# Storing the raw first up product and applying its activation beside the first down product; moving the second layer's weight combinations

## The chip, the cores and the metric

The kernel runs on 1 core of one Trainium2 chip. The metric is device time in microseconds (us) of one execution. Engines are named as in the profile: PE (matrix products, with PEld for the loads of its weights), DVE, ACT, POOL (element-wise work) and SP (here it only issues DMAs). ACT issues DMAs too: the stores.

## What is computed

```python
def _attn_ref(q, k, v, p):
    p_packed = sm_attn(p, k, v)
    return sm_attn(q, p_packed, p_packed)

def _moe_ref(x, w_in, w_out):
    h = x @ w_in
    g = h * np.cos(h)
    return g @ w_out

def _moe2_ref(x, w_in, w_out):
    h = x @ w_in
    g = np.where(h >= 1, h, np.where(h <= -1, 0.0, (h + 1) ** 2 / 4))
    return g @ w_out
```

Batch 8, 8 heads, 576 tokens, head width 64, 32 packed rows; 4608 tokens by 512 in all, and an inner width of 2048 in both layers. `reference` is attention, then the first layer (`moe_`), then the second (`moe2_`). Weights arrive as 64-bit floats and are cut to 32 bits on the chip.

## The kernel before, in words

A 32-bit value is cut by `split` (L66) into a high part, copied by ACT (L67), and a low part, a subtraction on POOL or DVE (L68). A product is three matmuls: high by high, high by low, low by high (`TERMS`).

**Attention phase with the first up product.** For each batch `n`, `stage1` and `stage2` make scores and softmaxes; the second attention's packed values are folded into the weights (`form_M`, `load_M` make `M[n, c]`), so that `up(n, hf, fp)` (L593) forms a 128x2x288 piece of h in 12 matmuls. There are 128 such items: 8 batches, 2 halves of the tokens, 8 pairs of inner blocks. The loop over `items` (L952) is written by hand: after each item it takes one step in each of the streams "load", "wt", "mat", "att" (Python generators), so these set what stands between two items. A scheduler then orders each engine's queue; `tc.high_priority` and `issue_after` shift pieces of it. The stream "wt" holds `cut_w_in` at first, and from batch 6 on `cut_w_out` (L502): 16 rows of blocks of the first layer's output weights, each brought in raw by SP, converted by `convert` (L124: ACT, four on DVE, POOL) and split.

h stays in one of three PSUM buffers `hps` until the activation h*cos(h) is done: `act_a` (L610) has ACT round h/2pi to an integer (L614) and DVE subtract it (L615); `act_b` (L620) has ACT take the sine (L623) and DVE multiply by h from PSUM (L624). The result goes to HBM as `g1T`.

**First down product** (`run_down1`, L775). 128 items of 24 matmuls (L792), each on one tile `g` loaded from `g1T` by SP, split by ACT and DVE (L786). Every eighth item ends a block: sums leave PSUM (L801, L803) and are stored as `yT`. After each item `step("wt")` takes one step of `combine` (L530): the second layer's products use seven combinations of blocks (a 2x2 scheme with 7 instead of 8 products, `ORDER_UP`, `KS`), and `combine` forms these from the weights. It has 16 units, 8 for `w_in2` (stored as `su`) and 8 for `w_out2` (`sd`). A unit is two raw loads (SP), two `convert`, four additions on DVE (L559 to L562), four `split` into tiles `pl`, and seven stores (SP).

**Second up product** (`run_up2`, L820). 8 batches times 4 pairs of inner blocks; each is a cycle of seven products of 12 matmuls (L743). Results leave PSUM by ACT (L716) and DVE (L721), go through `activate` (L724: ACT twice, DVE L729) and are stored as `gT`. Products that share a PSUM bank X, Y or Z add onto it, so PE waits there for DVE or ACT. `load_y` brings in the next batch once per four cycles and forms its seven sources on POOL and ACT.

**Second down product** (`run_down2`, L850): the same scheme with `sd`; 8 batches of 7 products of 48 matmuls (L891).

## Time and profile before

| what | us |
|---|---|
| median of 3 runs (1750.95 to 1758.61) | 1755.22 |
| the profiled execution's own time | 1760.71 |
| its span, first to last instruction | 1758.9 |
| PE busy in the span | 1596.1 (91%) |
| DVE busy | 1126.6 (64%) |
| ACT busy | 918.6 (52%) |
| POOL busy | 522.9 (30%) |

The mean granted clock of PE over the span is 0.945 of full speed. PE's busy share is of little use by itself: its instructions overlap, and one that runs at the lower clock is as busy as one at full speed. PEld's share is close to 100% where PE runs at its full rate. The stages follow one another, so they are read apart: the attention phase from 0 to 551 us, the first down product to 1015, the second up product to 1378, the second down product to the end.

### The profile page before, as it was taken

What the parts mean: (1) busy time and instruction counts of PE and PEld (TensorE: products, weight loads), DVE (VectorE), ACT (ScalarE), POOL (GpSimd) and SP (SyncE); (2) the same over time, 40 slices, a digit from 0 to 9 for tenths busy, and PEclk for the clock granted to TensorE, in tenths of its full rate; (3) what the DMA queues carried; (4) which work ended last, traced back from release to release, by engine and by line L of the source; (5) the groups of instructions that cost most, each with busy time, mean ns of one, the idle gap of its engine ahead of it and who ended that gap; (6) DMA issues with size and microseconds to landing.
All of it is one profiled execution on the core that took longest, in us unless ns stands there. A gap on an engine that the chain in (4) does not pass through costs nothing. (4 is left out here: it accounts for less than half of the span.)

```text
span 1758.9 us, 28668 instructions
## 1 busy us (share of the span) xinstructions
PE 1596.1 (91%) x10846; PEld 1524.1 (87%) x10846; DVE 1126.6 (64%) x1611; ACT 918.6 (52%) x1478; POOL 522.9 (30%) x376
## 2 busy tenths in 40 slices
PE   8679888878764998998999999999999799999998
PEld 6458777777664998988899999999999799999998
DVE  4887456547898665767522246666666597778775
ACT  3467678757665333333322246766666444444443
POOL 2763233333464463545300114444443000000000
PEclk7779999989987999999999999999999899999999
DMA  7566785646657898887744443333335954444430
GB/s 227 154 195 199 216 239 191 214 138 196 199 168 240 259 344 286 266 277 236 216 122 116 164 188 135 130 136 135 129 135 219 387 168 130 137 133 135 135 109 34
DMA packets 174539, 326.96 MB, mean 186 GB/s; under 512 B 16192, under 2 KB 70464, under 8 KB 170816
## 3 DMA queue, kind: packets, MB, share of 16 engines
q1 hardware_dynamic: 120128, 230.73, 42.8%
q10 hardware_dynamic: 54272, 94.39, 14.4%
q8 instruction: 85, 1.39, 0.3%
q14 instruction: 54, 0.44, 0.1%
HBM read 184.55 MB, written 130.02 MB: 179 GB/s over the span
## 5 line engine op out<-in xcount | busy, mean ns | idle before, releaser
L68 DVE TENSOR_TENSOR r<-g,r 128x576 fp32r<-128x576 f32 x352 | 286.9, 824 | 232.6 <-ACT r L67 227.1
L67 ACT ACTIVATE r<-g 128x576 fp32r<-128x576 f32 x352 | 239.2, 683 | 312.5 <-PE psZ L891 70.6
L604 PE MATMUL hps<-at,m 128*128 128x288 f32 x1536 | 255.5, 322 | 52.9 <-DVE u L624 39.9
L604 PEld LDWEIGHTS hps<-at,m 128*128 128x128 f32 x1536 | 233.0, 207 | 73.6 <-issue 40.8
L792 PE MATMUL psZ<-r,wo 128*128 128x288 f32 x1536 | 213.8, 300 | 12.0 <-ACT r L67 6.5
L792 PEld LDWEIGHTS psZ<-r,wo 128*128 128x128 f32 x1536 | 209.9, 191 | 15.1 <-DVE r L68 7.9
L891 PE MATMUL psZ<-r,sw 128*128 128x288 f32 x1152 | 159.6, 297 | 2.7 <-DVE r L68 1.8
L891 PEld LDWEIGHTS psZ<-r,sw 128*128 128x128 f32 x1152 | 156.4, 189 | 3.2 <-DVE r L68 2.0
L729 DVE SCALAR_TENSOR_TENSOR t<-hh,t 128x576 f32<-128x576 f32 x128 | 113.7, 889 | 69.8 <-ACT t L728 69.7
L792 PE MATMUL psX<-r,wo 128*128 128x288 f32 x768 | 130.0, 303 | 27.3 <-ACT r L67 21.8
L68 POOL TENSOR_TENSOR ty<-td,ty 128x576 fp32r<-128x576 f32 x32 | 52.0, 1630 | 306.5 <-ACT ty L67 306.5
L792 PEld LDWEIGHTS psX<-r,wo 128*128 128x128 f32 x768 | 112.5, 192 | 31.3 <-ACT r L67 22.7
L727 ACT ACTIVATE t<-hh,half 128x576 f32<-128x576 f32 x128 | 98.7, 772 | 61.8 <-DVE hh L721 48.7
L792 PE MATMUL psY<-r,wo 128*128 128x288 f32 x768 | 125.4, 299 | 0.0
L615 DVE SCALAR_TENSOR_TENSOR u<-hps,u 128x576 f32<-128x576 f32 x128 | 95.3, 747 | 45.0 <-ACT u L614 44.6
L68 POOL TENSOR_TENSOR m<-ml,m 128x512 fp32r<-128x512 f32 x64 | 85.0, 1341 | 128.9 <-ACT m L67 116.5
L624 DVE TENSOR_TENSOR u<-hps,u 128x576 f32<-128x576 f32 x128 | 94.8, 746 | 34.9 <-ACT u L623 34.9
L891 PE MATMUL psX<-r,sm 128*128 128x288 f32 x768 | 107.1, 299 | 9.2 <-ACT r L67 9.0
L891 PEld LDWEIGHTS psX<-r,sm 128*128 128x128 f32 x768 | 104.9, 190 | 9.7 <-ACT r L67 9.2
L743 PE MATMUL psZ<-ty,sw 128*128 128x288 f32 x768 | 111.8, 296 | 0.1
L792 PEld LDWEIGHTS psY<-r,wo 128*128 128x128 f32 x768 | 111.6, 191 | 0.0
L623 ACT ACTIVATE u<-u,halfpi 128x576 f32<-128x576 f32 x128 | 98.1, 771 | 25.5 <-DVE u L615 25.3
(158 smaller groups left out, 2783.4 us busy)
## 6 DMA issues: line engine op xcount, KB each, us to landing
g1T<-u ACTq DMA_DIRECT2D x128, 288.0 KB, 3.2
g<-g1T SPq DMA_DIRECT2D x128, 288.0 KB, 4.1
gT<-t ACTq DMA_DIRECT2D x128, 288.0 KB, 2.1
g<-gT SPq DMA_DIRECT2D x128, 288.0 KB, 3.3
raw<-in_moe_w_in SPq DMA_DIRECT2D x32, 512.0 KB, 6.1
raw<-in_moe_w_out SPq DMA_DIRECT2D x32, 512.0 KB, 4.7
su<-pl SPq DMA_DIRECT2D x56, 256.0 KB, 5.0
sd<-pl SPq DMA_DIRECT2D x56, 256.0 KB, 4.1
```

The costliest lines, as they stand in the source:

```text
L67: nc.scalar.activation(out=hi, in_=src, func=AF.Copy)
L68: (eng or nc.gpsimd).tensor_tensor(out=lo, in0=src, in1=hi.bitcast(F32), op=ALU.subtract)
L604: nc.tensor.matmul(out=hps[:, j, :HB], lhsT=m[:, w, G, cs], rhs=x[:, G, y], start=(G == 0 and i == 0), stop=(G == 1 and i == 2),)
L615: nc.vector.scalar_tensor_tensor(out=u, in0=h, scalar=1 / (2 * PI), in1=ki, op0=ALU.mult, op1=ALU.subtract)
L623: nc.scalar.activation(out=u, in_=u, func=AF.Sin, scale=2 * PI, bias=halfpi)
L624: nc.vector.tensor_tensor(out=u, in0=h, in1=u, op=ALU.mult)
L727: nc.scalar.activation(out=t, in_=h, func=AF.Relu, scale=0.5, bias=half)
L729: nc.vector.scalar_tensor_tensor(out=t, in0=h, scalar=1.0, in1=t, op0=ALU.max, op1=ALU.min)
L743: nc.tensor.matmul(out=ps[:, i], lhsT=s[:, d, w, cs], rhs=t[:, d, y], start=first and d == n == 0, stop=d == 1 and n == 2, skip_group_chec ...
L792: nc.tensor.matmul(out=acc[d // 2][:, d % 2], lhsT=wo[f // 4, w][:, f % 4, ds], rhs=r[:, y, k], start=f == n == 0, stop=f == NFT - 1 and n ...
L891: nc.tensor.matmul(out=ps[:, j], lhsT=s[:, f % 4, w, j * 128:j * 128 + 128], rhs=r[:, y, k], start=first and f == n == 0, stop=f == 7 and ...
```

## The change

1. `up` no longer applies the activation. One instruction copies h from PSUM (ACT for even `fp`, DVE for odd) and the raw h is stored as `h1T`.
2. `run_down1` loads h, and applies the activation there in SBUF: `act_a` three items ahead, `act_b` two, `split` one.
3. `combine` leaves `run_down1`. The units of `w_in2` go to the attention phase, in the stream "wt", from item 33 on (`cut_w_out` gets a stream of its own, "wo"); those of `w_out2` go to the second up product, one step after each product on X or Y.
4. A unit is spread over 11 steps instead of 6. Its tiles shrink: two raw buffers instead of four, one `pl` instead of two; the sums `pc` share a buffer with raw. `p1` has two buffers instead of three, `u` three instead of four. `load_v` takes the second half of v into the one buffer, later than before.

```diff
-    def combine(units):
-        def load(src):
-            raws = []
-            for x in range(2):
-                raw = prep[0].tile([128, 2, 256, 2], I32, tag="raw", name="raw", bufs=4)
...
+    def combine(units, slow):
+        def load(src, x):
+            raw = prep[0].tile([128, 2, 256, 2], I32, tag="raw", name="raw", bufs=2)
...
-                convert(raw, a[:, o])
+                convert(raw, a[:, o], last_act)
+                yield
                 store()
-                yield
-            if u + 1 < len(units):
-                nxt = load(units[u + 1][0])
-            s = prep[0].tile([128, 4, 256], F32, tag="pc", name="pc")
+            s = prep[0].tile([128, 4, 256], F32, tag="raw", name="pc", bufs=2)
+            raws = [load(following, 0)] if following else []
...
+            yield
             for k, n in ((0, 2), (2, 1), (3, 2), (5, 2)):
-                hl = prep[0].tile([128, 2, 2, 256], F32R, tag="pl", name="pl", bufs=2)
+                hl = prep[0].tile([128, 2, 2, 256], F32R, tag="pl", name="pl")
...
-                split(hl[:, 0, :n], hl[:, 1, :n], x)
-                store()
+                with behind(last_act):
+                    split(hl[:, 0, :n], hl[:, 1, :n], x)
...
                 yield
+                store()
+                if k < 5:
+                    for _ in range(slow - 1):
+                        yield
+            if following:
+                raws.append(load(following, 1))
+            yield
...
-        HS[n, hf, fp] = hps[:, :, :HB]
...
+        u = wk.tile([128, 2, HB], F32, tag="u", name="u", bufs=3)
+        with tc.high_priority(offset=PRI_MAIN):
+            if fp % 2:
+                nc.vector.tensor_copy(out=u, in_=hps[:, :, :HB])
+            else:
+                last_act[:] = [nc.scalar.activation(out=u, in_=hps[:, :, :HB], func=AF.Copy).ins]
+        late_store(h1T[fp, :, 2 * n + hf], u)
...
     def run_down1():
...
-        streams["wt"].append(combine([*units_up(), *units_down()]))
...
+        def act_a(i):
+            if i < B * 16:
+                t = turns[i] = pt.tile([128, 2, HB], F32, tag="t", name="t")
+                ki = t.bitcast(I32)
+                nc.scalar.activation(out=ki, in_=G1[i], func=AF.Copy, scale=1 / (2 * PI), bias=0.25)
+                nc.vector.scalar_tensor_tensor(
+                    out=t, in0=G1[i], scalar=1 / (2 * PI), in1=ki, op0=ALU.mult, op1=ALU.subtract
+                )
+
+        def act_b(i):
+            if i < B * 16:
+                t = turns[i]
+                nc.scalar.activation(out=t, in_=t, func=AF.Sin, scale=2 * PI, bias=halfpi)
+                nc.vector.tensor_tensor(out=t, in0=G1.pop(i), in1=t, op=ALU.mult)
+
+        def part(i):
+            if i < B * 16:
+                r = parts[i] = dn1["r"].tile([128, 2, 2, HB], F32R, tag="r", name="r1")
+                split(r[:, 0], r[:, 1], turns.pop(i), nc.vector)
+
+        for i in (0, 1, 2):
+            act_a(i)
+            if i:
+                act_b(i - 1)
+        part(0)
         for i in range(B * 16):
...
-            g = G1.pop(i)
-            r = dn1["r"].tile([128, 2, 2, HB], F32R, tag="r", name="r1")
-            split(r[:, 0], r[:, 1], g, nc.vector)
+            load_h1(i + 7)
+            part(i + 1)
+            act_b(i + 2)
+            act_a(i + 3)
+            r = parts.pop(i)
...
-            step("wt")
...
+        prep[:] = [pool("prep")]
+        last_act.clear()
+        streams["wt"].append(combine(units_down(), 2))
...
                     product_up(p, f, o, st)
+                    if o[0] != "Z":
+                        step("wt")
...
         if i == n_first + 1:
             drain("wt")
...
+            prep[:] = late
+            streams["wt"].append(combine(units_up(), 2))
         if n == B - 2 and fp == 0 and hf == 0:
-            streams["wt"].append(cut_w_out())
+            streams["wo"].append(cut_w_out())
...
```

How the queues stand is shown at three places. The first is DVE in the middle of the attention phase: `hps` is the PSUM piece of h, `u` its copy in SBUF, `pa`, `raw` and `pc` are the tiles of `combine`. Before:

```order
L615 SCALAR_TENSOR_TENSOR u<-hps,u 128x576
L238 TENSOR_REDUCE mx_3304<-s_3303 128x1
L624 TENSOR_TENSOR u<-hps,u 128x576
L239 TENSOR_SCALAR mx_3304<-mx_3304 128x1
L615 SCALAR_TENSOR_TENSOR u<-hps,u 128x576 x2
L247 TENSOR_SCALAR rs_3392<-sm_3390 128x1
L248 RECIPROCAL rs_3392<-rs_3392 128x1
L249 TENSOR_SCALAR s_3303<-s_3303,rs_3392 128x576
L624 TENSOR_TENSOR u<-hps,u 128x576
```

and now:

```order
L609 COPY u<-hps 128x576
L131 TENSOR_SCALAR pa<-raw 128x512
L132 SCALAR_TENSOR_TENSOR pa<-raw,pa 128x512
L343 STREAM_TRANSPOSE x<-psB 128x288
L135 TENSOR_SCALAR raw<-pa 128x512
L136 SCALAR_TENSOR_TENSOR raw<-raw 128x512
L609 COPY u<-hps 128x576
L551 TENSOR_TENSOR pc<-pa 128x256
L552 TENSOR_TENSOR pc<-pa 128x256
L553 TENSOR_TENSOR pc<-pc,pa 128x256
L554 TENSOR_TENSOR pc<-pa,pc 128x256
```

Two DVE instructions per item became one per two items, and the combination's ten stand between them.

The second place is DVE from the last items to the start of the first down product; `w_...` is a block of the first layer's output weights, `h_...` a loaded tile of raw h. Before:

```order
L131 TENSOR_SCALAR w_4661<-raw 128x512
L624 TENSOR_TENSOR u<-hps,u 128x576
L132 SCALAR_TENSOR_TENSOR w_4661<-raw,w_4661 128x512
L135 TENSOR_SCALAR raw<-w_4661 128x512
L136 SCALAR_TENSOR_TENSOR raw<-raw 128x512
L131 TENSOR_SCALAR pa<-raw 128x2x256
L132 SCALAR_TENSOR_TENSOR pa<-raw,pa 128x2x256
L135 TENSOR_SCALAR raw<-pa 128x512
L131 TENSOR_SCALAR pa<-raw 128x512
L136 SCALAR_TENSOR_TENSOR raw<-raw 128x512
```

and now:

```order
L131 TENSOR_SCALAR w_4632<-raw 128x512
L132 SCALAR_TENSOR_TENSOR w_4632<-raw,w_4632 128x512
L135 TENSOR_SCALAR raw<-w_4632 128x512
L136 SCALAR_TENSOR_TENSOR raw<-raw 128x512
L773 SCALAR_TENSOR_TENSOR t<-h_4661,t 128x576
L773 SCALAR_TENSOR_TENSOR t<-h_4663,t 128x576
L781 TENSOR_TENSOR t<-h_4661,t 128x576
L773 SCALAR_TENSOR_TENSOR t<-h_4665,t 128x576
L781 TENSOR_TENSOR t<-h_4663,t 128x576
L773 SCALAR_TENSOR_TENSOR t<-h_4667,t 128x576
L68 TENSOR_TENSOR r_4829<-t,r_4829 128x576
L781 TENSOR_TENSOR t<-h_4665,t 128x576
```

Where one block of weights (its last three rows) and the first combination stood between the last item and the first split, the last copy of h now stands sixteen rows, four blocks of weights, ahead of the first L773, and the activation of the first items stands ahead of the first split.

The third place is DVE in the second up product; `p_...` is the copy of X1's result, `q`, `u`, `hh` are sums out of PSUM, `t` is the activation. Before, one cycle:

```order
L729 SCALAR_TENSOR_TENSOR t<-hh,t 128x576
L721 TENSOR_TENSOR hh<-psZ,q 128x576
L729 SCALAR_TENSOR_TENSOR t<-hh,t 128x576
L721 TENSOR_TENSOR hh<-psY,u 128x576
L729 SCALAR_TENSOR_TENSOR t<-hh,t 128x576 x2
L721 TENSOR_TENSOR hh<-psZ,p_10458 128x576
L721 TENSOR_TENSOR u<-psZ,p_10609 128x576
L721 TENSOR_TENSOR q<-psY,p_10609 128x576
L729 SCALAR_TENSOR_TENSOR t<-hh,t 128x576 x2
L721 TENSOR_TENSOR hh<-psZ,q 128x576
L721 TENSOR_TENSOR hh<-psY,u 128x576
```

and now:

```order
L708 TENSOR_TENSOR q<-psY,p_10379 128x576
L716 SCALAR_TENSOR_TENSOR t<-hh,t 128x576
L131 TENSOR_SCALAR pa<-raw 128x512
L132 SCALAR_TENSOR_TENSOR pa<-raw,pa 128x512
L135 TENSOR_SCALAR raw<-pa 128x512
L136 SCALAR_TENSOR_TENSOR raw<-raw 128x512
L708 TENSOR_TENSOR hh<-psZ,q 128x576
L716 SCALAR_TENSOR_TENSOR t<-hh,t 128x576
L708 TENSOR_TENSOR hh<-psY,u 128x576
L551 TENSOR_TENSOR pc<-pa 128x256
L552 TENSOR_TENSOR pc<-pa 128x256
L553 TENSOR_TENSOR pc<-pc,pa 128x256
```

The conversions and additions of `combine` stand between the sums that free PE's banks.

## Rows read from the trace of the kernel before

**Rows 1.** Busy time by stretch: start:end, length, busy us by engine (instructions), PE clock, DMA.

```profile
core 0: us, PE busy (x) PEld busy (x) DVE busy (x) ACT busy (x) POOL busy (x), PEclk, DMA share, GB/s
68.00:216.00 148.00, 123.04 (x645) 103.78 (x644) 106.79 (x162) 96.45 (x169) 65.58 (x51) 0.85 0.63 192
216.00:445.00 229.00, 196.34 (x1152) 172.20 (x1152) 136.60 (x220) 162.23 (x277) 79.94 (x64) 0.94 0.65 199
445.00:551.00 106.00, 72.67 (x420) 65.75 (x419) 95.41 (x137) 71.04 (x113) 58.80 (x44) 0.89 0.57 182
...
569.00:860.00 291.00, 270.94 (x1921) 264.14 (x1919) 194.12 (x273) 110.51 (x186) 143.09 (x99) 0.97 0.85 275
860.00:1015.00 155.00, 154.73 (x1150) 154.73 (x1151) 39.99 (x54) 36.40 (x55) 5.61 (x4) 0.99 0.49 148
...
1040.00:1350.00 310.00, 309.95 (x2323) 309.47 (x2322) 194.84 (x251) 216.63 (x326) 121.44 (x74) 1.00 0.37 133
```

**Rows 2.** The chain that ended last, second down product: start us, us, what.

```profile
1427.20 6.40 PE psZ L891 x48
```

**Rows 3.** Waits of PE, 68 to 551 us: waiting, releaser, us, times, longest.

```profile
PE hps L604 <- DVE u L624: 39.9, 26, 6.0
PE psB L454 <- ACT cp L460: 10.1, 7, 3.6
```

**Rows 4.** Waits of PE, 445 to 551 us.

```profile
PE hps L604 <- DVE u L624: 29.6, 17, 6.0
```

**Rows 5.** Waits of all engines, 568 to 860 us.

```profile
ACT pl L67 <- DMA sd<-pl: 41.0, 21, 5.0
ACT pl L67 <- DMA su<-pl: 27.7, 13, 5.2
...
PE psX L792 <- ACT r L67: 21.8, 4, 19.1
```

**Rows 6.** Waits in SP's DMA queue, 568 to 860 us.

```profile
SPq L543 <- POOL pl L68: 74.4, 44, 4.8
```

**Rows 7.** Groups by line, whole run: out<-in, forms, count, busy us, mean ns, idle before.

```profile
L67 ACT ACTIVATE r<-g 128x576 fp32r<-128x576 f32 x352 | 239.2, 683 | 312.5 <-PE psZ L891 70.6 <-PE psY L792 65.8 <-PE psZ L792 54.4
...
L729 DVE SCALAR_TENSOR_TENSOR t<-hh,t 128x576 f32<-128x576 f32 x128 | 113.7, 889 | 69.8 <-ACT t L728 69.7
...
L623 ACT ACTIVATE u<-u,halfpi 128x576 f32<-128x576 f32 x128 | 98.1, 771 | 25.5 <-DVE u L615 25.3
L615 DVE SCALAR_TENSOR_TENSOR u<-hps,u 128x576 f32<-128x576 f32 x128 | 95.3, 747 | 45.0 <-ACT u L614 44.6
L624 DVE TENSOR_TENSOR u<-hps,u 128x576 f32<-128x576 f32 x128 | 94.8, 746 | 34.9 <-ACT u L623 34.9
...
L614 ACT ACTIVATE u<-hps 128x576 int32<-128x576 f32 x128 | 81.8, 644 | 39.1 <-PE hps L604 34.3 <-DMA g1T<-u 1.6 <-DVE e L267 0.8
...
L623 ACT ACT_TABLE_LOAD x15 | 19.2, 1283 | 0.3
...
L801 DVE COPY o<-psZ 128x576 f32<-128x576 f32 x8 | 6.0, 752 | 16.5 <-PE psZ L792 16.5
```

**Rows 8.** Busy time, 551 to 863 us, of tiles pa, pl; lines L129, L136, L139.

```profile
551.00:863.00 312.00, 90.94 (x160) 16.55 (x32) 89.08 (x64) 0.94 0.84 275
...
551.00:863.00 312.00, 36.55 (x64) 85.67 (x64) 0.94 0.84 275
...
551.00:863.00 312.00, 22.47 (x33) 0.94 0.84 275
...
551.00:863.00 312.00, 27.84 (x34) 0.94 0.84 275
...
551.00:863.00 312.00, 55.84 (x34) 0.94 0.84 275
```

**Rows 9.** Groups by line, DVE alone, 640 to 850 us, then 870 to 1000 us.

```profile
L68 DVE TENSOR_TENSOR r<-g,r 128x576 fp32r<-128x576 f32 x57 | 60.1, 1059 | 49.3 <-ACT r L67 46.2 <-DMA sd<-pl 3.1
...
L68 DVE TENSOR_TENSOR r<-g,r 128x576 fp32r<-128x576 f32 x40 | 30.3, 757 | 85.3 <-ACT r L67 85.3
```

**Rows 10.** DMA issues, whole run: count, KB each, median us to landing.

```profile
su<-pl SPq DMA_DIRECT2D x56, 256.0 KB, 5.0
```

145 lines of the change are left out of this document (58 added, 87 removed).

## The prediction, on record before the changed kernel had run

> **What bounds the kernel now.** I cut the span at the stages and read busy time by stretch first. The full rate comes from the chain that ended last: 48 matmuls of the second down product take 6.40 us, 0.1333 us each [rows 2]. A stretch whose PEld is about 100% busy runs at that rate. So do 860 to 1015 us (154.7 of 155) and 1040 to 1350 us (309.5 of 310), where the granted clock is 1.00 of its upper level, 2.4 GHz. The attention phase does not, nor the first part of the first down product [rows 1]. The reader should see two different losses there.
>
> From 68 to 551 us PE has 645 + 1152 + 420 rows; even at 0.1333 us each they are 296 us of 483, and the fp32 and 512-column ones are longer. The waits of PE say what it lacks: 39.9 us for L624, the last step of the activation, which frees a PSUM piece of h; 10.1 us for a copy in the forming of M [rows 3]. Of the 39.9, 29.6 lie in the last 32 items, from 445 us [rows 4], and there DVE is busy 95.4 us of 106 [rows 1]: that stretch is bound by DVE. From 216 to 445 us (items 33 to 96) no engine is full; PEld is busy 172 of 229, the clock averages 0.94 of full speed.
>
> The first down product needs 128 x 24 = 3072 matmuls, 409.6 us, and takes 446 (569 to 1015). As 860 to 1015 is at full rate, all 36 us are lost before 860, while `combine` runs. The waits of that stretch show how: ACT stands 41.0 + 27.7 us for the stores of the `pl` tiles, and the split that PE needs is queued behind [rows 5].
>
> **The change, part by part.** *Activation out of the attention phase.* Per item go 644 + 771 ns of ACT and 747 + 746 ns of DVE [rows 7], in all 181 and 191 us. One copy comes back: on ACT 644 ns (the same instruction with another scale), on DVE 752, the price of the nearest copy of 576 columns from PSUM [rows 7]; 64 of each, 41 and 48 us. The order shows the table loads of ACT falling from 30 to 2 at 1.283 us: 36 us more off ACT. Also a PSUM piece is now held for one instruction, where it was held for four that alternate between two engines; with three pieces that is worth more than the busy time.
>
> *Combinations into it.* A unit costs, from 16 units between 551 and 863 us [rows 8]: DVE 90.94 / 16 + 2 x 27.84 / 34 = 7.3 us; ACT 36.55 / 16 + 2 x 22.47 / 33 = 3.6; POOL 85.67 / 16 + 2 x 55.84 / 34 = 8.6. Eight units bring 59, 29 and 69 us; all run after item 33. Their 56 stores of 256 KB [rows 10] and 16 loads of 512 KB are 23 MB; over some 300 us that adds 75 GB/s to 199, about the 275 that the first down product carries now [rows 1]. The stores stand in SP's queue with the loads for attention; SP waited 74.4 us in 44 waits for POOL's half of `pl` [rows 6], so a load behind one may come 2 to 5 us late. I take no price for that by itself: the loads stand a step or more ahead.
>
> By stretch. From 445 us DVE had 95.4; 32 items give back 47.8, 16 copies bring 12.0, 2.3 units (63 of the steps are past at item 96, 11 a unit) bring 16.8: 76.4. At the same 90% occupancy that is 85 us, a gain of 21. The gap to the next stage, 551 to 569 us, stays: the two raw loads that ACT waited for go, but four blocks of weights are now left behind the last copy of h (order, second place), and the first items' activation, some 5 us of ACT and DVE, stands ahead of the first split. I charge 2: gain 19. From 216 to 445 us DVE goes to 136.6 - 95.6 + 24.1 + 5.7 x 7.3 = 107, and POOL to 79.9 + 49 = 129. Neither binds, so PE's waits decide; bounds are 0 and 75 (1152 rows at full rate). I take 15, near the low end, since the copies for M, the splits of M and the softmax stay and now share queues with the combinations. From 68 to 216 us 32 items leave and nothing comes: bounds 0 and 62, I take 15, as the conversions of `w_in`, which stay, set the pace there. Sum **-49**, bounds -10 and -80.
>
> *First down product.* Per item 3.2 us of PE. DVE now has 3 x 757 ns (without POOL beside it [rows 9]) = 2.3 us, ACT 644 + 771 + 683 = 2.1 [rows 7]: 71% and 66%, three items deep, with no DMA to wait for except loads seven ahead. The 36 us go but for a few at the start: **-33**, bounds -36 and -20. The extra instructions are hidden by PE; without that cover they would be 128 x 1.5 us.
>
> *Combinations in the second up product.* This has the smallest slack. A cycle of seven products is 84 x 0.1333 = 11.2 us, and DVE is busy 194.8 / 310 of it, 7.0 us; ACT 216.6 / 310, 7.8; POOL 121.4 / 310, 4.4 [rows 1]. Four steps a cycle and 11 a unit make 2.75 cycles per unit, so DVE gets 2.7 more, ACT 1.3, POOL 3.1: 87%, 82% and 67% during 22 of 32 cycles. DVE also slows beside POOL: a subtraction with both inputs in SBUF takes 1059 ns against 757 alone [rows 9], and L729 (mean 889 [rows 7]), in whose stretch POOL is 39% busy, is of that kind. With L729 at 1060 DVE has 10.4 us a cycle, 93%. Behind each conversion on DVE stand the sums that free banks X, Y, Z; such a sum has two products, 3.2 us, before PE wants the bank, and four conversions in a row (order, third place) are about 2.6 us. So some cycles stall. The nearest price is the first down product: 36 us for 16 units, 2.3 a unit, at DVE 67% busy. DVE is fuller here, the pace slower (11 steps for 6). I take 3.1 a unit: **+25**, bounds +5 (the steps fall into DVE's idle time) and +50 (twice and more that price).
>
> The rest, start and second down product with its wait for `sd`, is unchanged: 0. Sum -49 - 33 + 25 = **-57**. The profiled execution's own time is 1760.7 us, span 1758.9, 5.5 above the median of the runs, so about 1704 by its scale; against the median of 1755.2 I forecast **1698 us**.
>
> **A rule against it.** The split's subtraction takes 1.4 times as long beside POOL [rows 9], where POOL is busy 143 us of 291 [rows 1]. My +25 takes that as a longer duration. The Trainium skill, page "SBUF — State Buffer", section "Who interferes with whom", states more: a DVE instruction with two SBUF inputs and a POOL instruction that reads SBUF exclude each other for their whole length. By that rule the sum on the shared port counts, as in rival 2, and the forecast would be 1718. The rows show the slowdown, not yet a full port.
>
> **The rivals.** *1. Attention does not shorten.* Its items lose work, but what PE waits for is the chain of scores, M and softmax, into which POOL's 69 us are put (POOL busy goes from 35 to 56% of 216 to 445 us). For it: no engine is full there. Against: the 39.9 us on L624. Then -10 for -49: 1737.
>
> *2. The second up product is bound by DVE and POOL together.* If they exclude each other, a cycle needs POOL's 7.5, four L729 at the 757 ns of a lone two-input instruction [rows 9], 3.0, and of the unit's 2.7 on DVE all but some conversions, I take 2.2: 12.7 us for 11.2, 22 times: +33, with waits +45. Against it: POOL's own 7.5 already contains waiting. Then 1755 - 49 - 33 + 45 = 1718.
>
> *3. The single `pl` tile stops ACT: slower.* With two tiles ACT stood 68.7 us for 64 splits. With one, each split in the second up product waits until POOL has made the low part (85.67 / 64 = 1.3 us [rows 8]), SP has issued and the store has landed (5.0 us [rows 10]): 6.3, while two steps take 5.6 us of PE. ACT is in order, and the copies that free bank X stand behind. The gain of 82 is eaten if each of 32 splits costs PE 2.6 us, and from 2.9 on the kernel is over 0.5% slower; at 4 it ends at 1755 - 82 + 128 = 1801. Against it: DMA is lightly used there (share 0.37 [rows 1]), so a store lands sooner.
>
> *4. Attention runs near PE's rate.* Freed PSUM pieces let PE run ahead, the clock stays up: -85 in attention, +10 in the second up product: 1755 - 85 - 35 + 10 = 1645.
>
> **How the numbers follow.** Forecast 0.57, rival 1 0.13, rival 2 0.14, rival 3 0.06, rival 4 0.10. Within 0.5% (about what a measurement of this kernel can tell) is 1746 to 1764. Faster: 0.57 + 0.14 + 0.10 and half of rival 1, 0.87; same: the other half, 0.07; slower: rival 3, 0.06. The range is 1655 to 1740: it takes in rivals 1 and 2 and the bounds of my own terms except their extremes together, and leaves out rival 3, about half of 4 and the upper part of 1, about 0.18.
>
> **What would show it.** Right: PE's waits for the freeing of `hps` nearly gone; the first matmul of the first down product near 520 us; that product in 410 to 416 us with PEld at 99%; the second up product in 380 to 395 us instead of 363, with PE waiting for DVE's sums. Wrong: attention above 540 us, PE waiting for M or scores (rival 1); ACT's split of `pl` waiting for `sd` stores by over 60 us in the second up product (rival 3). The second up product under 370 us would make my +25 wrong, and one above 410 the sign of its neighbours' gain irrelevant.

## The result: 0.6% slower

The changed kernel takes 1764.77 us (median of 11 runs, 1757.94 to 1771.14), the kernel before 1753.65 beside it (11 runs, 1747.31 to 1759.54): ratio 1.0061, 95% interval 1.0039 to 1.0082. The forecast was 1698 us.

Busy time by stretch of the changed kernel follows; the columns are those of [rows 1]. The stages now end elsewhere, so the stretches answer to those rows as follows: 67 to 196 us holds items 0 to 31 ([rows 1] has item 32 in its first stretch too), 196 to 414 items 32 to 95, 414 to 533 the rest; 533 to 571 is the gap, 571 to 982 the first down product, and 1040 to 1350 lies in the second up product in both.

```profile
core 0: us, PE busy (x) PEld busy (x) DVE busy (x) ACT busy (x) POOL busy (x), PEclk, DMA share, GB/s
67.00:196.00 129.00, 106.98 (x580) 92.18 (x580) 71.82 (x101) 47.86 (x94) 63.80 (x48) 0.84 0.65 206
196.00:414.00 218.00, 197.17 (x1202) 172.47 (x1202) 123.33 (x205) 97.97 (x206) 115.94 (x94) 0.97 0.84 276
414.00:533.00 119.00, 80.63 (x436) 70.67 (x435) 79.60 (x100) 43.60 (x74) 75.61 (x56) 0.83 0.81 261
533.00:571.00 38.00, 0.42 (x2) 0.42 (x2) 25.67 (x33) 15.12 (x23) 18.53 (x14) 0.55 0.67 230
571.00:860.00 289.00, 288.77 (x2156) 288.42 (x2156) 214.63 (x291) 196.15 (x292) 8.52 (x5) 0.99 0.43 124
860.00:982.00 122.00, 122.00 (x917) 122.00 (x916) 76.74 (x103) 72.16 (x107) 8.96 (x6) 1.00 0.43 137
1040.00:1350.00 310.00, 290.60 (x2104) 286.50 (x2104) 243.16 (x301) 216.80 (x338) 169.34 (x109) 0.98 0.54 183
```

The first down product is full, as forecast (PEld 288.42 of 289). The second up product is not (2104 matmuls in 310 us where [rows 1] have 2323). What was not forecast are the third and fourth rows: PE is busy 81 us of 157. The waits of PE in that stretch, 414 to 571 us (who waited, for whom, us in total, times, longest):

```profile
PE psX L807 <- ACT r L67: 37.7, 1, 37.7
PE hps L602 <- ACT at L67: 14.1, 1, 14.1
PE hps L602 <- DVE u L609: 7.2, 4, 2.3
PE hps L602 <- ACT u L611: 4.2, 2, 2.1
```

The freeing of the pieces of h costs 11.4 us where it cost 29.6 [rows 4], but 14.1 us for `at` of the last batch are new, and the wait for the first split of the first down product, 19.1 us before, has doubled. By stages, from the start of each one's first matmul to the next one's, in the two profiled executions:

| | before | after | difference | forecast |
|---|---|---|---|---|
| item 96 starts at | 445.5 | 413.7 | -31.8 | -30 |
| item 96 to the last up matmul's end | 103.9 | 119.2 | +15.3 | -19 with |
| from there to the first down product | 19.1 | 37.7 | +18.6 | the gap |
| first down product | 446.8 | 411.6 | -35.2 | -33 |
| second up product | 363.2 | 397.5 | +34.3 | +25 |
| second down product | 376.3 | 376.0 | -0.3 | 0 |

These sum to +1 us. The medians differ by 11, since the profiled execution of before was 7 us above its median and that of after 3 below. Stretches whose code is the same vary among the traces of this study: the changed second up product takes 396.6 to 406.0 us (ten kernels, mean 401.6), the one without units 361.4 to 367.7 (four, mean 364.6). The price of the units there is therefore nearer to 37 than to 34. The attention phase of after stands unchanged in e5, e8, e9 and f3 below: in these five item 96 starts between 410.5 and 420.4 us, and from there to the first down product it is 155.9 to 159.1 us. So the start of a single item or product says little within 10 us, and the length of that stretch is good to about 3.

### The profile page after: what moved, and what is told of

The parts are those of the page before. It is cut to its first block, busy times and chain, and to the rows that moved or that the text cites. A ratio compares the mean times of both kernels' runs of the same rounds, so it can differ in the third digit from the quotient of the medians.

```text
span 1759.9 us, 28596 instructions
## 1 busy us (share of the span) xinstructions
PE 1584.2 (90%) x10846; PEld 1514.2 (86%) x10846; DVE 1210.4 (69%) x1675; ACT 930.8 (53%) x1514; POOL 519.6 (30%) x376
## 5 line engine op out<-in xcount | busy, mean ns | idle before, releaser
L602 PE MATMUL hps<-at,m 128*128 128x288 f32 x1536 | 243.6, 313 | 42.1 <-ACT at L67 15.3
L602 PEld LDWEIGHTS hps<-at,m 128*128 128x128 f32 x1536 | 223.8, 199 | 59.0 <-ACT at L67 17.1
L67 ACT ACTIVATE r<-g 128x576 fp32r<-128x576 f32 x224 | 153.7, 687 | 184.6 <-PE psZ L909 72.6
L68 DVE TENSOR_TENSOR r<-g,r 128x576 fp32r<-128x576 f32 x224 | 166.3, 754 | 71.1 <-ACT r L67 71.1
L807 PE MATMUL psZ<-r,wo 128*128 128x288 f32 x1536 | 206.1, 296 | 0.0
L68 DVE TENSOR_TENSOR r<-t,r 128x576 fp32r<-128x576 f32 x128 | 99.8, 779 | 95.0 <-ACT r L67 94.9
L807 PE MATMUL psX<-r,wo 128*128 128x288 f32 x768 | 124.3, 297 | 37.9 <-ACT r L67 37.7
L716 DVE SCALAR_TENSOR_TENSOR t<-hh,t 128x576 f32<-128x576 f32 x128 | 123.9, 969 | 48.1 <-ACT t L715 48.0
L67 ACT ACTIVATE r<-t 128x576 fp32r<-128x576 f32 x128 | 87.8, 686 | 101.5 <-PE psZ L807 52.4
L730 PEld LDWEIGHTS psZ<-ty,sw 128*128 128x128 f32 x768 | 106.6, 190 | 10.1 <-DVE hh L708 9.8
L773 DVE SCALAR_TENSOR_TENSOR t<-h,t 128x576 f32<-128x576 f32 x128 | 99.0, 774 | 14.5 <-ACT t L772 5.4
```

The costliest lines, as they stand in the source:

```text
L67: nc.scalar.activation(out=hi, in_=src, func=AF.Copy)
L68: (eng or nc.gpsimd).tensor_tensor(out=lo, in0=src, in1=hi.bitcast(F32), op=ALU.subtract)
L602: nc.tensor.matmul(out=hps[:, j, :HB], lhsT=m[:, w, G, cs], rhs=x[:, G, y], start=(G == 0 and i == 0), stop=(G == 1 and i == 2),)
L716: nc.vector.scalar_tensor_tensor(out=t, in0=h, scalar=1.0, in1=t, op0=ALU.max, op1=ALU.min)
L730: nc.tensor.matmul(out=ps[:, i], lhsT=s[:, d, w, cs], rhs=t[:, d, y], start=first and d == n == 0, stop=d == 1 and n == 2, skip_group_chec ...
L773: nc.vector.scalar_tensor_tensor(out=t, in0=G1[i], scalar=1 / (2 * PI), in1=ki, op0=ALU.mult, op1=ALU.subtract)
```

## Experiments

All are read in one table (us; "cut" is the end of the last block of `w_out` by `cut_w_out`, POOL's last row of `wo`; the products are counted to the next one's first matmul). In some expectations the second up product is counted to another matmul: 383 to 392 there is 397 to 405 here, and 404 to 413 is 396 to 406.

| kernel | item 96 | last up ends | cut | first down product from | it takes | second up product | ratio to before (interval) |
|---|---|---|---|---|---|---|---|
| before | 445.5 | 549.4 | 561.0 | 568.5 | 446.8 | 363.2 | 1 |
| after | 413.7 | 532.9 | 563.7 | 570.6 | 411.6 | 397.5 | 1.0061 |
| e1 | 421.3 | 539.8 | 568.1 | 575.1 | 412.1 | 404.4 | 1.0064 (1.0044-1.0084) |
| e3 | 430.3 | 548.1 | 571.9 | 582.4 | 411.8 | 404.8 | 1.0147 (1.0117-1.0177) |
| e4 | 403.9 | 508.5 | 532.4 | 538.8 | 443.2 | 404.5 | 1.0071 (1.0045-1.0097) |
| e5 | 417.0 | 535.2 | 566.8 | 576.1 | 447.1 | 365.9 | 1.0087 (1.0054-1.0119) |
| e6 | 415.6 | 538.7 | 555.6 | 566.1 | 412.4 | 401.9 | 1.0057 (1.0036-1.0078) |
| e7 | 422.3 | 544.2 | 557.8 | 564.8 | 412.4 | 399.7 | 1.0003 (0.9987-1.0018) |
| e8 | 420.4 | 538.8 | 569.7 | 577.0 | 412.9 | 389.7 | one run |
| e9 | 415.2 | 534.6 | 564.9 | 571.7 | 412.9 | 376.9 | one run |
| f1 | 418.3 | 542.7 | 555.7 | 562.7 | 412.1 | 396.6 | 1.0011 (0.9995-1.0028) |
| f2 | 408.4 | 517.4 | 524.3 | 536.7 | 437.4 | 401.6 | 1.0013 (0.9987-1.0039) |
| f3 | 410.5 | 529.2 | 559.5 | 566.4 | 411.7 | 395.7 | 1.0061 (1.0040-1.0082) |
| g1 | 422.5 | 551.2 | 537.5 | 568.0 | 411.4 | 406.0 | 1.0103 (1.0080-1.0126) |
| g2 | 418.5 | 529.7 | 519.3 | 557.5 | 412.4 | 398.0 | one run |
| **g3** | 447.0 | 547.7 | 545.6 | 552.0 | 440.9 | 361.4 | **0.9904 (0.9889-0.9920)** |
| g4 | 402.4 | 514.0 | 499.4 | 525.1 | 451.7 | 399.1 | 1.0051 (1.0034-1.0067) |
| h1 | 408.3 | 521.1 | 506.3 | 532.3 | 487.8 | 367.7 | 1.0078 (1.0050-1.0105) |
| h2 | 416.1 | 543.9 | 540.1 | 568.7 | 412.5 | 399.1 | 1.0044 (1.0027-1.0061) |

### The end of the attention phase

In the trace of after, SP's queue has loads of `sm` (L653) among the raw loads of `w_out`; ACT stood 8 us in order behind a store of h for DVE's copy; and combinations still ran there. Each was taken away alone.

e1:

```diff
-                for o in ORDER_UP[:6]:
-                    load_su(0, o)
+                with tc.issue_after(loads[20]):   # 21st load of h1T
+                    for o in ORDER_UP[:6]:
+                        load_su(0, o)
```

> One edit on the changed kernel: the twelve loads of the first combined blocks for the second up product (sm<-su, L653) are queued on SP behind the 21st load of h1T, so they leave the end of the attention phase. Theory Q (the loads of sm, each of which waits on SP for PE to free a tile of M, hold back the raw loads of w_out behind them, and so the cutting of w_out and the first load of h): the gap between the last up matmul and the first matmul of the first down product falls from 37.7 to 18-22 us, the kernel is 12 to 18 us faster than the changed kernel, some 1748-1753. Theory D (the end is long because DVE and POOL have the remaining combinations beside the cutting of w_out): SP's waits at L653 move, the cutting ends at most 4 us earlier, and the time stays within 5 us of 1765. Theory S (the 14 us wait at 474 us for the freeing of hps decides): time as the changed kernel's, the wait stays.

The gap stayed at 35.3 us and nothing was won. The loads did move; theory Q falls for this place.

e3:

```diff
-            if fp % 2:
-                nc.vector.tensor_copy(out=u, in_=hps[:, :, :HB])
-            else:
+            if True:
                 last_act[:] = [nc.scalar.activation(out=u, in_=hps[:, :, :HB], func=AF.Copy).ins]
```

> One edit on the changed kernel: all copies of raw h from PSUM run on ACT, none on DVE, so that ACT's store of h never waits for a copy that stands behind combinations in DVE's queue. Theory S (the 14.1 us wait of PE near 474 us came from ACT standing in order at a store for DVE's copy, with the softmax behind it): that wait is gone or under 4 us, the items from 413.7 us to the last up matmul take about 105 instead of 119 us. ACT gets 64 x 0.65 = 42 us more over 480, DVE 48 less, so the middle of attention moves by under 5 us either way. If the gap to the first down product is bound by SP's queue (theory Q), what is won here is partly lost there: the kernel is 5 to 14 us faster. If the wait comes from DVE's load and not from ACT's place in order (theory D): the wait shrinks to 7-10 us, and 3 to 7 us are won.

A miss: the wait for `at` grew to 19.5 us and the kernel lost 0.9% more. ACT's standing behind that store is not the cause alone. In after the softmax's exponential (L355) starts 8.4 us after POOL has finished its input (L350), in e3 1.1 us after; yet there the rest of the chain to `at` takes longer, with conversions and sums of the combinations between its steps on DVE.

e4:

```diff
+        # run_down1
+        streams["wt"].append(combine(units_up(), 2))
...
+            step("wt")
             if i == 13 * 8:
+                drain("wt")
...
-            streams["wt"].append(combine(units_up(), 2))
```

> One part of the change undone: the eight units of combinations for the second up product run in the first down product (11 steps a unit, one step an item) and none in the attention phase; those for the second down product stay in the second up product. Theories Q and D both expect the attention phase to end earlier: with su written late no sm load can be hoisted, and DVE, POOL lose 59 and 69 us there; last up matmul near 515-522 us, gap 19-22 us, first down matmul near 538 us, 33 us earlier. They tell what the combinations cost in attention altogether. The first down product then takes 411 us plus 8 units at the 0 to 2.3 us each of the kernel before, 411 to 430 us. Sum: 15 to 33 us faster than the changed kernel, 1732-1750. If the tail's length comes from what the activation left behind (neither Q nor D: for example from the clock or the order of the softmax), the attention phase ends where it does in the changed kernel and nothing is won.

The start of the first down product came where it was expected, 538.8 us and 32 earlier, but the first down product took 443.2, 32 more and beyond the 430 that I had allowed. Nothing was left of it: the eight units cost PE as much in the one place as in the other. This trace also disproves my own step. Neither the activation nor a combination runs here after item 96; start:end, length and busy us as above:

```profile
404.00:508.00 104.00, 77.75 (x438) 68.27 (x437) 64.41 (x85) 39.43 (x66) 61.46 (x47) 0.85 0.66 202
508.00:539.00 31.00, 0.73 (x5) 0.49 (x5) 23.79 (x32) 13.57 (x21) 15.17 (x11) 0.54 0.61 189
```

DVE falls from 95.41 us [rows 1] to 64.41, and the last two batches still take 104 us. So taking 31 us of DVE's work out of them bought nothing: DVE's share of 90% before did not tell how long they take. The second row is what follows the last up matmul, blocks of `cut_w_out` up to 532.4. In before, after, e1 and e3 to e7 the first matmul of the first down product follows the last block's cut by 6.4 to 10.5 us, wherever the last up matmul ended. In the order that the program writes, a block is two steps of one an item, and what is left at item 120 is written at once; the items became faster, the blocks did not. Three blocks' last rows stand behind the last up matmul in before, six in after. POOL's and ACT's rows at the end of after (start us, length, what, count, idle before and its releaser):

```profile
560.39 1.27 POOL L139 TENSOR_TENSOR w<-w,raw 128x512 f32<-128x512 f32 x1 [0.63 <-DVE raw L136]
562.40 1.26 POOL L68 TENSOR_TENSOR wo<-w,wo 128x512 fp32r<-128x512 f32 x1 [0.74 <-ACT wo L67]
```

```profile
557.66 0.63 ACT L67 ACTIVATE wo<-w 128x512 fp32r<-128x512 f32 x1 [1.69 <-POOL w L139]
561.70 0.63 ACT L67 ACTIVATE wo<-w 128x512 fp32r<-128x512 f32 x1 [3.40 <-POOL w L139]
564.65 1.41 ACT L772 ACTIVATE t<-h 128x576 int32<-128x576 f32 x2 [2.32 <-DMA h<-h1T]
566.07 1.28 ACT L780 ACT_TABLE_LOAD   x1
...
569.86 0.67 ACT L67 ACTIVATE r<-t 128x576 fp32r<-128x576 f32 x1
```

Behind the last block come the load of h (issued at 561.7, when POOL's L139 has read the last raw tile), the activation with its table load, and the split; PE starts at 570.58.

e6 and e7 give the cutting more steps, and e7 also ends the combinations before the last two batches:

```diff
-            streams["wt"].append(combine(units_up(), 2))
+            streams["wt"].append(combine(units_up(), 1))          # e7 only
...
-        for name in ("load", "wt", "wo", "mat", "att", "load", "mat", "att"):
+        for name in ("load", "wt", "wo", "mat", "att", "load", "wo", "mat", "att"):
+        # e7: ... + ("wt",) * (i % 2)
```

> One edit on the changed kernel: the cutting of w_out (16 blocks, two steps each) gets two steps per item instead of one. Theory W: the first down product starts late because this cutting, a serial chain per block (load, ACT, four DVE, POOL, ACT, POOL: 5.1 us a block after the last copy of h), is paced by the items, so that with the items now faster, eight blocks are left behind the last up matmul where the kernel before had two. Then with twice the steps the last block is cut before or near the last up matmul, the gap of 37.7 us falls to 12-20 us, and the items from 413.7 us on lose at most 8 us to it: 8 to 20 us faster than the changed kernel, 1745-1757. Theory D (the engines DVE, ACT and POOL together lack time from 414 to 570 us, whatever the order): the gap shrinks, but the last up matmul comes later by about as much, within 5 us of the changed kernel.

> Two edits on the changed kernel: the cutting of w_out at two steps per item, and the combinations of the attention phase faster (one step less after each store and three steps in two items), so that the eight units end before the last two batches, where the one before showed no cost for them: from item 64 to 96 the changed kernel took about 97 us and the kernel without these units about 104. Theory W: the first matmul of the first down product comes at 535-548 instead of 570.6 us, the kernel is 20 to 35 us faster, 1730-1745. Theory D (a unit costs PE some 3 to 4 us wherever it stands, as the one with the units in the first down product showed, 443 for 412 us): items 32 to 96 become longer by 15 to 20 us, and the whole gains under 15 us, 1750-1762.

e6 took 10 us off the gap, and the items from 96 on gave 4 back (123.1 us, where the five kernels with the attention of after have 118.2 to 119.4); its median is 1 us below the changed kernel's. In e7 the gap is 20.6 us and the kernel equals before. Both came out at the small end, as theory D has it: what leaves the gap comes back before it. f1 (e7 with the softmax of `stage2` and `weights_T` under `tc.high_priority`) changed nothing.

> The kernel with both early edits (w_out in two steps an item, combinations faster), and in it the softmax over the last stage's scores (maximum, POOL's subtraction, sums, POOL's products, the transposition and the split into at) ahead of other work, where only its exponential was. Theory C (between batches PE waits for this chain, which stands in DVE's and POOL's queues behind combinations and conversions: 10.7 us at batch 7 in the kernel with both early edits): that wait falls under 5 us, items from 422 us to the last up matmul take 114 instead of 122 us, and the first down product starts 5 to 10 us earlier: 0.3 to 0.6% faster than before. Theory D (DVE, POOL and ACT together lack the time): the wait moves to the copies of h and of M; under 3 us either way.

To see whether the cutting sets the start, g2 leaves half of it out, and g3 and h2 begin the same work eight items earlier and give it two steps an item from item 96 on:

```diff
+        # g2: eight blocks of w_out only, each used twice
-        for f in range(NFT):
+        for f in range(NFT // 2):
```

```diff
+        # g3 in the kernel before; h2 the same in after, with the stream "wo"
-            if n == B - 2 and fp == 0 and hf == 0:
+            if i == len(items) - 40:
                 streams["wt"].append(cut_w_out())
...
-        for name in ("load", "wt", "mat", "att") + ("load", "mat", "att"):
+        for name in ("load", "wt", "mat", "att") + ("load", "mat", "att") + ("wt",) * (n >= B - 2):
```

> The changed kernel, with only the first eight of the sixteen blocks of w_out cut; the first down product uses each of these twice, so its result is not the reference's. Matmuls and their number stay. Theory W: the cutting ends before the last up matmul, near 500 us, and the first down product starts 8-14 us after the last up matmul (h's load, activation and split), at 530-545 instead of 570.6 us. Theory D or S (the items' own waits): the last up matmul stays near 533 us or comes up to 8 us earlier, and the gap stays above 25 us.

> The kernel before, with the cutting of w_out begun eight items earlier (item 88) and two steps an item from item 96. Theory W: in it too the first down product begins 9.5 us after the last block is cut (559 us) and the items end at 549.4, so the gap of 19.1 us falls to 9-13 us and no further, because there the items themselves end late: 5 to 9 us faster than before, 0.3 to 0.5%. If DVE, 90% busy from 445 us, is what binds it, the items get later by as much as the cutting gets earlier, and nothing is won.

> One edit on the changed kernel, the one that made the kernel before 1% faster: w_out's cutting begun at item 88, two steps an item from item 96. Theory W alone: last block cut near 540, first down product 9 us later, 549-553 instead of 570.6: 15 to 20 us faster than the changed kernel, 1745-1750. Theory W2 (behind the cutting stands a second wait of about the same length: the combinations' last units with their single tile pl, whose stores wait on SP behind the loads of sm, as in the kernel with half of the cutting): the cutting ends earlier, the gap stays 25-35 us or the items end later, 0 to 8 us faster than the changed kernel.

g3 is the fastest kernel of this study: 1735.28 us, 1.0% faster than before, by more than I expected. PE's last up matmuls and the first of the first down product in g3 (the wait in brackets was 19.05 us before):

```profile
544.02 3.64 PE L604 MATMUL hps<-at,m 128*128 128x288 f32 x24 [1.02 <-DVE u L624]
552.00 1.30 PE L792 MATMUL psX<-r,wo 128*128 128x288 f32 x4 [4.34 <-DVE u L624]
```

The items end where they did (547.7 for 549.4) and the gap falls from 19.1 to 4.3 us: in the kernel before, the cutting set the start, and its engines had room for it earlier. In the changed kernel the same edit wins at most 3 us (h2, 1763.94). There the cutting ends at 540.1 and the gap stays at 24.8 us. g2 shows what stands behind it, on ACT:

```profile
533.58 0.42 ACT L67 ACTIVATE pl<-pa 128x256 fp32r<-128x256 f32 x1 [2.21 <-DMA h<-h1T]
...
549.28 0.63 ACT L67 ACTIVATE pl<-pc 128x512 fp32r<-128x512 f32 x1 [15.29 <-DMA su<-pl]
549.82 2.39 ACT L772 ACTIVATE t<-h 128x576 int32<-128x576 f32 x4
```

and on SP in the same stretch:

```profile
532.36 0.32 SPq L653 DMA_DIRECT2D sw<-su  x1
536.88 15.29 SPq L535 DMA_DIRECT2D su<-pl  x3
554.25 0.33 SPq L653 DMA_DIRECT2D sw<-su  x1
```

The first h loads were issued at 517 us already. ACT waits 15.29 us for the store of the combinations' single tile `pl`, and the activation of the first h stands behind that split in order. This is the mechanism of my third rival, in a place where I had not looked for it. The store is not issued late: it leaves SP at 536.9, 2.1 us after POOL has made the low half, and lands 12.3 us later, where [rows 10] have 5.0. Five loads of `sm` and `sw`, 1 MB each, were issued between 528.6 and 532.4 us and took 8.3 to 16.2 us to land. h2 shows the same: its store of `pl`, issued at 552.4, lands after 8.0 us, and ACT waits 8.42 for it.

```profile
560.52 0.63 ACT L67 ACTIVATE pl<-pc 128x512 fp32r<-128x512 f32 x1 [8.42 <-DMA su<-pl]
561.06 2.38 ACT L772 ACTIVATE t<-h 128x576 int32<-128x576 f32 x4
```

Meanwhile the DMA engines are nearly full and the others stand almost still, first in g2, then in h2 (columns as in the result):

```profile
533.00:549.00 16.00, 0.00 (x0) 0.00 (x0) 0.41 (x1) 0.42 (x1) 0.72 (x1) 0.50 0.93 385
541.00:561.00 20.00, 2.86 (x22) 2.63 (x20) 1.51 (x2) 1.69 (x4) 0.72 (x1) 0.64 0.92 336
```

In after, where the cutting still runs from 541 to 561 us, the DMA share is 0.49. So behind the cutting stands the DMA traffic. That the loads of `sm` are what delays the store is read from these rows, not tried: holding them back was tried only where the cutting still bound (e1).

g1 is e7 with the same early cutting:

> The kernel with both early edits, and the cutting of w_out begun eight items earlier (at item 88; one step an item up to item 96, two from there). Theory W (the end of that cutting sets the start of the first down product, whatever the last up matmul does): the last block is cut at 535-545 instead of 556 us, the gap falls from 20.6 to 8-14 us, the first down product starts at 548-556 instead of 564.8, and the kernel is 8 to 16 us faster than that one, 1738-1747, 0.4 to 0.9% faster than before. Theory D (engines full): the cutting ends earlier but the last up matmul later, within 4 us of 1754.

A miss: the cutting ended at 537.5, but the last up matmul at 551.2, and it is the slowest but one. With combinations, cutting and copies all ahead of time, the items wait for DVE's and ACT's copies, and these wait for the stores that free the three tiles `u` of raw h: 17.6 us on DVE and 12.9 on ACT between 422 and 568 us.

### What a unit of combinations costs

e5 moves the other eight units:

```diff
+        # run_down1
+        streams["wt"].append(combine(units_down(), 3))
...
+            step("wt")
...
-        streams["wt"].append(combine(units_down(), 2))
```

> One part of the change undone in another place: the eight units of combinations for the second down product run in the first down product (12 steps a unit), and the second up product has none. My theory of the second up product (the 34 us more come from the combinations' work on DVE, POOL and ACT there, whose sums free the banks): it returns to 361-366 us, and the first down product rises from 411 to 413-430 us (DVE then has 2.3 + 0.5 us of 3.2 an item). Net 15 to 32 us faster than the changed kernel, 1733-1750. Rival: the second up product is longer for another reason that came with the change (its loads of sm done at another time, the slow clock after a stall, one tile less for p1): it stays at 385-397 us and the first down product rises, so the kernel is slower than the changed one by up to 20 us.

The second up product returns to 365.9 us, and the first down product rises by 35.5: 4.4 us a unit there, as e4's 31.6 make 4.0, and in the second up product 4.3 by the profiled pair, 4.6 by the means. Moving a unit wins nothing.

e8 and e9 leave out one engine's part of the units in the second up product:

```diff
+        # e8, units_down only
-        nc.gpsimd.tensor_tensor(out=a, in0=a, in1=lf, op=ALU.add)
...
-                    split(hl[:, 0, :n], hl[:, 1, :n], x)
+                    nc.scalar.activation(out=hl[:, 0, :n], in_=x, func=AF.Copy)
...
+        # e9, units_down only: the four nc.vector calls of convert and the four tt of combine left out
-        nc.gpsimd.tensor_tensor(out=a, in0=a, in1=lf, op=ALU.add)
+        nc.gpsimd.tensor_tensor(out=a, in0=hf, in1=hf, op=ALU.add)
```

> In the second up product the combinations are made without POOL: the low words are not added and the low halves are not made (the high half is stored in both places), so the second product's weights lack their low parts. DVE's and ACT's work stays. Theory P (shared port: DVE's sums with both inputs in SBUF slow down beside POOL): the second product's up part falls from 383-392 us to 358-370 us, and the mean of the subtraction at L716 from 960 to 890 ns or less. Theory V (DVE's own 7 us a unit, in order ahead of the sums that free PE's banks): it stays at 378-392 us, L716 below 900 ns all the same.

> In the second up product the combinations are made without DVE: its conversions and its four sums are left out (POOL adds the high words to themselves, and the split takes blocks of those), so the second product's down weights are not those of the reference. POOL's and ACT's work stays. Theory V: the up part falls from 383-392 us to 353-366 us. Theory P (the port): it stays above 372 us, since POOL still reads two tiles in SBUF beside DVE's sums, and L716 stays near 950 ns. Theory A (ACT's place in order behind the single tile of the split): it stays above 378 us in both of these kernels.

Against the mean of 401.6 us, e8 saves 12, e9 25, of 37; each is one run, and the ten kernels of that mean lie between 396.6 and 406.0. DVE's own part weighs most, POOL's less; ACT's part was not left out alone. DVE's row of the turn's third step, 1010 to 1340 us, in after, e8, e9 and e5 (which has no unit here):

```profile
L716 DVE SCALAR_TENSOR_TENSOR t<-hh,t 128x576 f32<-128x576 f32 x108 | 109.0, 1009 | 37.1 <-ACT t L715 37.0
```

```profile
L724 DVE SCALAR_TENSOR_TENSOR t<-hh,t 128x576 f32<-128x576 f32 x110 | 98.6, 896 | 46.0 <-ACT t L723 45.9
```

```profile
L720 DVE SCALAR_TENSOR_TENSOR t<-hh,t 128x576 f32<-128x576 f32 x114 | 113.3, 997 | 83.7 <-ACT t L719 82.9 <-DMA gT<-t 0.7
```

```profile
L716 DVE SCALAR_TENSOR_TENSOR t<-hh,t 128x576 f32<-128x576 f32 x107 | 95.2, 890 | 57.5 <-ACT t L715 57.5
```

POOL's part makes the mean of this instruction 0.11 us longer, whether or not DVE has units: in e9 it is still 997 ns, and yet 25 us are back, for DVE idles 83.7 us before it.

f3 cuts a unit finer on DVE, f2 gives the splits more room, g4 spreads the units more thinly as well:

```diff
+        # f3, units_down only: a step after two of convert's four DVE instructions, and after two of the four sums
...
+        # f2 = e4, w_out in two steps an item, and
-            part(i + 1)
-            act_b(i + 2)
-            act_a(i + 3)
+            part(i + 2)
+            act_b(i + 3)
+            act_a(i + 4)
...
+        # g4 = f2 and f1's priority, cutting from item 88, combine(..., 3) for both
```

> One edit on the changed kernel: in the second up product a unit's work on DVE is cut finer, two instructions a step where there were four (14 steps a unit for 11), so that the sums that free PE's banks stand behind 1.5 us instead of 3. Theory L (what costs PE is a sum late behind a row of conversions, not DVE's time): the up part falls from 404-413 us to 380-390 us, 20 us faster than the changed kernel. Rival (DVE's and POOL's time itself): 398 us or more, as the units then merely reach further into the stretch.

> The kernel with the units for the second up product in the first down product, and two edits: w_out's cutting at two steps an item, and the activation, its load and the split one item further ahead of PE (the split two items ahead where it was one). Theory L (8 units cost 31 us in the first down product though DVE has 2.3 + 0.5 us of 3.2 an item, because a split only one item ahead is late whenever a unit's conversions stand before it): the first down product falls from 443 to 413-422 us, and the gap from 30 to 18-24: 25 to 40 us faster than the one it is made from, 1727-1742, that is 0.7 to 1.6% faster than before. Rival (throughput: DVE with POOL beside it is full during the units): 432 us or more, only the gap's part is won, 1748-1757.

> The changed kernel with everything that looked useful: units for the second up product in the first down product, one item further ahead, spread over 14 steps a unit; units for the second down product over 14 steps a unit in the second up product; the softmax ahead of other work; w_out's cutting begun at item 88. Theory W and spreading: last up matmul near 510, first down product from 520-528 us in 425-435 us, second up part in 385-400 us: 1722-1740, 1 to 2% faster than before. If a unit's cost does not depend on the spreading (4 us each wherever it stands), the first down product takes 437-443 us and the second up part 404-412: 1740-1752.

f3's second up product is at 395.7 us, 1 below the fastest of the ten without this edit, and its median is the changed kernel's: no gain. f2 won 6 of the 31 us, g4 lost 8 more than e4. So a late split or a row of conversions is at most a small part of it. In the second up product e9 points to DVE's work itself; that it is the amount of work in the first down product too is argued from DVE's 91%, not tried. Busy time in f2 while the units run, and after them:

```profile
660.00:760.00 100.00, 93.03 (x679) 90.54 (x678) 91.37 (x127) 68.17 (x110) 27.94 (x19) 1.00 0.77 249
...
860.00:980.00 120.00, 120.00 (x902) 120.00 (x901) 72.36 (x97) 68.77 (x102) 13.17 (x9) 1.00 0.46 152
```

h1 is the first part of the change alone, all sixteen units in the first down product, and the early cutting:

```diff
+        # run_down1
+        streams["wt"].append(combine([*units_up(), *units_down()], 1))
...
-        streams["wt"].append(combine(units_down(), 2))
...
-        if n == B - 2 and fp == 0 and hf == 0:
+        if i == len(items) - 40:
             streams["wo"].append(cut_w_out())
```

> The first part of the change alone: raw h stored, activation in the first down product, all sixteen units of combinations in the first down product as before (8 steps a unit), none in attention or in the second up product; w_out's cutting begun at item 88, as in the kernel before with that edit, against which it stands (first down product from 552 us in 441 us, second up part 370 us, 1735). Theory E (a unit costs PE about 4 us beside the activation, 2.3 without it): last up matmul near 510, first down product from 520-527 us in 470-485 us, second up part 371: 1727-1745, so nothing won or lost by the move within 0.5%. Rival (in attention the activation cost its full 80 us of DVE from item 33 on, and beside PE it is free): first down product in 445 us from 520: 1705-1715.

The first down product starts 19.7 us earlier than in g3 and takes 46.9 more: 1769.49 us, by the two ratios 1.8% above g3. PE's waits there are 22.8 and 12.0 us for DVE's part of the split (570 to 1000 us):

```profile
PE psX L809 <- DVE r L68: 22.8, 24, 3.0
PE psZ L809 <- DVE r L68: 12.0, 15, 1.4
```

A unit costs 4.7 us beside the activation ((487.8 - 412) / 16), 2.2 without it ((446.8 - 412) / 16): the first part of the change moves DVE work into the stage where the units need DVE. Nor does the attention phase keep what it gives. Item 96 starts 38.7 us earlier than in g3, but 12.1 of these are lost in the items from there on (112.8 us for 100.7) and 6.9 in the gap (11.2 for 4.3), in which the first activation now stands. The stretch from item 96 to the first down product, g3's row first, then h1's:

```profile
447.00:552.00 105.00, 69.77 (x413) 62.19 (x412) 96.56 (x134) 72.13 (x114) 62.04 (x44) 0.91 0.61 193
408.00:532.00 124.00, 80.91 (x439) 70.39 (x439) 88.27 (x100) 50.17 (x82) 72.61 (x53) 0.79 0.67 214
```

DVE and ACT have less to do there in h1, and it takes 19 us longer. PE, with 439 instructions for 413, is busy 81 us instead of 70, at a mean granted clock of 0.79 of the upper level instead of 0.91; how much of the 19 us that makes, no run separates.

## Why the prediction was wrong, step by step

- **Items up to 96: right, with the halves shifted.** I forecast -15 and -15; item 32 starts 4 us earlier, item 96 32 us.
- **The failed step: "From 445 us DVE had 95.4 ... At the same 90% occupancy that is 85 us, a gain of 21. The gap to the next stage ... stays ... gain 19."** Measured: +34 from item 96 to the first down product (156.9 for 123.0), a miss of 53 us. DVE's work up to the last up matmul came out near the forecast, 79.6 us (414 to 533 us) for 76.4, though more of the cutting lies behind it than before. What failed is that the time follows it: DVE is 67% busy there, not 90. I took DVE's high share for the bound, and the gap for a constant of 18 us, though it was the end of a second chain, the cutting of `w_out`, which ended 12 us after the items. The runs showed three things in its place. Without combinations there (e4) the stretch takes 134.8 us, so about 22 of the 34 are theirs; with them the 16 blocks of `w_out` take 128 us, from POOL's first `wo` to its last, where e4 needs 110 and before 103. With the cutting begun early as well (h1) it takes 124.0. And that is no shorter than before, and 19 longer than in g3, which has the old items with the same early cutting: the gain that I expected from DVE comes in none of these runs. I had charged 2 us for the "four blocks of weights" that "are now left behind the last copy of h". Blocks of weights did end last in after, but they are not the whole loss: without that wait (h2) at most 3 us are won, since the DMA traffic stands behind it, to which I had given no price.
- **First down product: right**, -35 for -33. That PE hides the activation needs a DVE free of units; h1 shows the price otherwise.
- **Second up product: right in kind, too small.** +34 in the profiled pair, 37 by the means, for +25, within its bounds of +5 and +50. My 3.1 us a unit measured 4.3 to 4.6.
- **Rival 2** priced DVE and POOL as excluding each other. Instruction by instruction they do (last section): L716's median stays at 759 ns and its longest is 2034. So says the Trainium skill, page "SBUF — State Buffer", section "Who interferes with whom"; the trace agrees. My +25 read the mean of [rows 9] as a general slowdown; its kind was wrong, since fewer than half of the 108 are lengthened, and that the sum came out near is partly luck. POOL's price is what e8 gets back, about 12 of 37 us. The larger part, 25 by e9, is DVE's own work in the units, which rival 2 had not at this size.
- **Rivals.** Rival 1's symptom came true for the last two batches (14.1 us for `at`, no shorter), not for the items before. Rival 3 did not occur where it was put: ACT waited 13.0 us for `sd` in the second up product, not 60; but its mechanism is the second wait at the end of attention (g2, h2), by the time that the store takes to land. Rival 4 fell.
- **The signs.** The waits on `hps` shrank, the first down product took 411.6 us, the second up product passed the 395 by 3. The decisive sign, a first matmul near 520 us, is missed by 50.

Left open: what holds the last two batches at 101 to 113 us even without combinations (e4, h1, and with the old items g3). In e4 10.8 us of it are one wait for `at`; the granted clock of that stretch is 0.85, between PE's two levels. In e4 the softmax's exponential of that batch starts 3.6 us after POOL has finished its input, behind a copy on ACT that waits 4.0 us for a store of raw h. Not tried: a fourth tile `u`, a second `pl` tile in the attention phase, and e1's edit together with the early cutting.

## What to carry to other kernels

A gap at the end of a stage is not a constant: find the chain that ends last there, here a low-priority preparation paced by another loop's items, before crediting a stage with what its busiest engine saves. A two-line edit that started this chain eight items earlier and gave it two steps an item won 1%, where moving 190 us of DVE's work won nothing. Ask too what stands right behind that chain: here full DMA engines. And before work is moved into another engine's idle time, price it by a row in which it already runs beside what it will meet: a unit cost 2.2 us beside the plain split and 4 to 5 beside anything fuller.

## What was not expected of the hardware

Beside POOL a DVE instruction with both inputs in SBUF is not a little slower each time: most run at their own pace, and the others last until a POOL instruction has ended. Of L716's 108 between 1010 and 1340 us, 62 take under 800 ns and 40 take 1000 or more; before, with POOL 39% busy instead of 55%, it is 18 of 111 (L729, 1040 to 1350 us). The view of one line gives the shortest, median and longest duration in ns, then the first and last start; L716 in the second up product of after, and the 256-column sum L552 in its whole run:

```profile
L716 DVE SCALAR_TENSOR_TENSOR t<-hh,t x108: 739/759/2034, 1010.5 to 1338.9; 128x576 f32<-128x576 f32 x108
```

```profile
L552 DVE TENSOR_TENSOR pc<-pa x16: 409/418/2351, 235.6 to 1224.6; 128x256 f32<-128x256 f32 x16
```

The longest of each, beside what POOL did (start us, length; POOL's first row is two instructions of 1.4 us in succession):

```profile
1291.63 2.82 POOL L68 TENSOR_TENSOR ty<-td,ty 128x576 fp32r<-128x576 f32 x2
1293.04 2.03 DVE L716 SCALAR_TENSOR_TENSOR t<-hh,t 128x576 f32<-128x576 f32 x1 [1.33 <-ACT t L715]
```

```profile
471.12 2.33 POOL L350 TENSOR_TENSOR x<-x,mx 128x1152 f32<-128x1152 f32 x1
471.38 2.35 DVE L552 TENSOR_TENSOR pc<-pa 128x256 f32<-128x256 f32 x1
```

L716 ends 0.62 us after POOL's second instruction, L552 0.28 after POOL's only one. It is the same for all 40: each ends 0.61 to 0.63 us after a POOL instruction that it had met, whatever its own start. So such an instruction lasts as long as POOL still needs, and most of its own time on top. The means, 1009 for L716, mix the two kinds, and a price taken from a mean holds only where POOL is as busy as in the row it came from.
